# Attention and mixture-of-experts kernel: the order and the PSUM banks of the score chunks change, with the opening and the issue of some weights

## The chip, the cores and the metric

One Trainium2 chip, one core of it. The metric is device microseconds of one execution, the median over runs. TensorE is called PE here, VectorE DVE, ScalarE ACT, GpSimd POOL; SP is SyncE, which only issues DMAs. A row of weight loads has the engine name PEld: loading weights runs beside PE's matmuls.

## The reference, cut to what matters

```python
# attention: q, k, v are (4, 12, 448, 64); cap = 30
scores = (q @ k.T) / 8
scores = cap * tanh(scores / cap)
attn = exp(scores - max); attn /= attn.sum(-1) + 1e-9
x = (attn @ v)              # -> (1792, 768), the heads side by side
# mixture of experts: 8 experts, w1 (8, 768, 1024), w2 (8, 1024, 768)
logits = x @ w_gate; e = argmax(logits)
gate = softmax(logits)[e]; eom = sigmoid(x @ w_output_gate)[e]
out = gate * eom * (relu(x @ w1[e]) @ w2[e])
```

## The kernel before, in words

The work has two stages. Attention runs over NU = 24 units: a unit is two heads of one batch, six units are a batch. The experts' stage then takes blocks of 128 rows that chose one expert, and smaller "rests", through w1 and w2.

**One unit.** The 448 keys of a head are three chunks of 128 and 64 more. `qk(u, s)` for s = 0, 1, 2 makes the scores of 128 keys of both heads: 6 matmuls that use 64 rows of the array each (one head in each half of the array, three passes for the high and low parts of K and Q), into two PSUM banks. `qk(u, 3)`, the half chunk, takes the last 64 keys of both heads together: 3 matmuls over all 128 rows, one bank. ACT applies tanh to each chunk from PSUM into the SBUF tile `pt`, and then one exp over the whole tile (`expo`). `pv(u, c)` multiplies with the values, 4 pieces, into one PSUM tile `u`, which `u_evac` copies to SBUF. The kernel is a software pipeline: in the loop's turn for unit u the order is qk(u), DVE's transposes and splits of K and Q for later units (`turn_next`), part of the row sums of unit u-1 on POOL (`presum`), exp(u), pv(u-1), `sums` of units u-3 and u-2 on PE when u is odd, the copy of pv(u-1), then the rest of the row sums on POOL. Each engine works through its own instructions in the order in which they are written.

**Slots.** The router of a batch is cut into pieces (`end_of_batch`), hung into the turns of the units that follow, at the places named "f", "g", "h", "q", "e" of the loop. `gate_mm` and `gate_out` (PE, ACT), `sums_out` (ACT), `sums_tr` and `recips` (PE, DVE), `gate_tr` and `gate_mul` (PE, DVE), `logits`, `choose`, `rank_mm`, `place`, `enter`, and `rws`, which turn and store the rows of x (`row_tr` and `row_out` by PE and DVE, `row_v` by DVE alone).

**Banks.** PSUM has 8 banks. One is the tile `t` of the transposes by DVE, one is `sm` (the row sums of a batch). The other six before the change, from unit NN = 3 on: A and B of two banks each for the scores, C of one bank for the half chunk (`s3`), D of one bank for `u`. Chunks 0 and 2 go to A, chunk 1 to B; the order is 0, 1, half, 2. The router's tiles take B and C in turn (`extra`). Units 0 to 2 run on three rotating pairs of banks (tags r0 to r2) in the order 0, 1, 2, half.

```python
for s in range(NK) if u < NN else (0, 1, NK):
    qk(u, s)
...
    qk(u, NK if u < NN else 2)
```

**The copy of u.** For u >= UACT it is ACT's, after exp in its queue; for smaller u it is DVE's.

**The opening.** K and Q of units 0 to 2 are loaded in natural layout, by SP's and ACT's queue, and turned by PE (`nat_k`, `nat_q`, `first_planes`).

**Rests' weights.** Three rests have weights of their own (`OWN`), loaded by POOL's queue into buffers of their own (`rh`): after each chunk of the experts' matmuls `between` calls `pump`, which issues one such load when a buffer is free (`hraw` counts the issued, `hused` the used).

Of the kernel before, what the change touches and what calls it, by code (L numbers as in the profile page):

```python
# [9 lines left out]
F32 = mybir.dt.float32  # L10
# [12 lines left out]
def tile_kernel(ctx: ExitStack, tc, q, k, v, cap, w_gate, w_ogate, w1, w2, out):  # L23
    nc = tc.nc
    B, H, S, D = q.shape
    NT, DM = out.shape
    E, _, DFF = w1.shape
# [27 lines left out]
    WARM = (32, 7)  # L55
    RB = 7
    SP0 = 3
    UACT = 8
    TURN = {0: (0, 0), 1: (0, 0), 3: (2, 1), 5: (2, 1), 6: (2, 1), 7: (2, 1), 13: (2, 1), 19: (2, 1),
            20: (0, 0), 21: (0, 0), 22: (0, 0)}  # L60
    KD = DM // 128
# [49 lines left out]
    def load_natural(dst, src, n, m, engs, lo=0):  # L111
        for j in range(2):
            o = lo if j == 0 else 0
            engs[j].dma_start(out=dst[:, 0:n, j], in_=src[j, o:o + n * m].rearrange("(c p) d -> p c d", c=n))

    def load_nat(u, engs):
        (k0, q0), k_, q_ = nat[u], heads(k, u), heads(q, u)
        load_natural(k0, k_, NK, 128, engs, T0)
        r0, n = u * S, NP * S + SK
        engs[1].dma_start(out=k0[0:64, NK], in_=k.rearrange("b h s d -> (b h s) d")[r0:r0 + 2 * n]  # L120
                          .rearrange("(j r) d -> r j d", j=2)[0:T0])
        load_natural(q0, q_, NCH, CP, engs)

    KT, QT = (0, 1, 4), (2, 3, 5)
    kview = [raw1[i].rearrange("p (h r a) -> p h r a", h=2, a=32) for i in KT]
# [167 lines left out]
    def copy(act, dst, src):  # L293
        if act:
            nc.scalar.activation(out=dst, in_=src, func=ACTF.Copy)
        else:
            nc.vector.tensor_copy(out=dst, in_=src)
# [39 lines left out]
    def first_planes(u, mid=lambda: None):  # L337
        ts, (main, *tails) = k_parts(u, nat_k(u))
        if u:
            copy(False, main[0], main[2])  # L340
            minus(main[1], main[2], main[0])
        mid()
        q_, (q0,) = q_parts(u, nat_q(u))
        if u:
            copy(False, q0[0], q0[2])
        else:
            copy(True, main[0], main[2])
            copy(True, q0[0], q0[2])
            minus(main[1], main[2], main[0])
            scales()  # L350
        minus(q0[1], q0[2], q0[0])
        for x, z, y in tails:
            copy(False, x, y)
            minus(z, y, x)
        pl[u] = ts + q_

    def t_k(u):
        pl[u] = planes_of(k_parts(u, turned(ldk.pop(u), SK + 128)))
# [24 lines left out]

    def scores(name, z):
        ring[0] += 1
        return ps_s[0].tile([128, 2, 512], F32, tag="AB"[z] if begun else f"r{ring[0] % 3}", name=name)

    ready = {}

    def single(name, z):  # L390
        if not begun:
            return scores(name, z)[:, 0]
        return ready.pop(z, None) or ps_s[0].tile([128, 512], F32, tag="CD"[z], name=name)

    begun = []

    def fixed():
        begin.close()
        ps_s[0] = att.enter_context(tc.tile_pool(name="ps_s", reuse_waits="tile", bufs=1, space=PSUM))
        begun.append(1)  # L400
        for z in (1, 0):
            ready[z] = ps_s[0].tile([128, 512], F32, tag="CD"[z], name=("s3", "u")[z])

    spare = [0]

    def extra(name):
        spare[0] ^= 1
        return scores(name, 1)[:, 0] if spare[0] else single(name, 0)

    def nat_k(u):  # L410
        pk = tbank([128, S], "tk0")
        for c in range(NK + 1):
            n = min(128, S - c * 128)
            nc.tensor.transpose(pk[:, c * 128:c * 128 + n], nat[u][0][0:n, c].rearrange("p j d -> p (j d)"), ident[0:n, 0:n])
        return pk
# [6 lines left out]

    def qk(u, s):
        KH, KL, QH, QL = pl[u]
        if s == 0:
            pt[u] = ptp.tile([128, 2 * NK + 1, S], F32, tag="pt", name="pt")
        n = 2 if s < NK else 1
        sl = slice(s * 128, (s + 1) * 128)
        if s < NK:
            ps = scores("s", s % 2)  # L430
            for i, (x, y) in enumerate(((KH, QH), (KL, QH), (KH, QL))):
                for j in range(2):
                    h = slice(64 * j, 64 * j + 64)
                    nc.tensor.matmul(ps[:, j, 0:S], lhsT=x[h, sl], rhs=y[h], start=(i == 0), stop=(i == 2))  # L434
            ps = ps[:, :, 0:S]
        else:
            ps = ps_m.tile([128, S], F32, tag="sm", name="s3m") if u == 1 else single("s3", 0)[:, 0:S]
            for i, (x, y) in enumerate(((KH, QH), (KL, QH), (KH, QL))):
                nc.tensor.matmul(ps, lhsT=x[:, SK:], rhs=y, start=(i == 0), stop=(i == 2))
            ps = ps.unsqueeze(1)  # L440
        nc.scalar.activation(out=pt[u][:, 2 * s:2 * s + n], in_=ps, func=ACTF.Tanh, scale=icap)  # L441
# [4 lines left out]
    def pv(u, c):  # L446
        P = pt[u]
        V = vvs[u // 2 % 2][:, u % 2]
        if c == 0:
            ups[u] = (single("u", 1) if u < NU - 1 else scores("u", 1)[:, 0])[:, 0:S]  # L450
        for j in range(2):
            nc.tensor.matmul(ups[u][64 * j:64 * j + 64], lhsT=V[:, c, j, :], rhs=P[:, 2 * c + (j if c < NK else 0)],  # L452
                             start=(c == 0), stop=(c == NK))
# [49 lines left out]
    def end_of_batch(b):  # L503
        def bank(shape, name, m=False):
            if b == B - 1:
                return tbank(shape, name)
            if m:
                return ps_m.tile(shape, F32, tag="sm", name=name)
            x = extra(name)[0:shape[0], 0:math.prod(shape[1:])]
            if len(shape) == 2:  # L510
                return x
            k = "abc"[:len(shape) - 1]
            return x.rearrange(f"p ({' '.join(k)}) -> p {' '.join(k)}", **dict(zip(k, shape[1:])))
# [3 lines left out]
            nc.scalar.activation(out=ssb, in_=smt.pop(b), func=ACTF.Identity, bias=epsc)  # L517

        def sums_tr():
            ps = rt["trec"] = bank([CP, NCH, 4, 32], "trec", b == B - 2)  # L520
            for c in range(NCH):
                nc.tensor.transpose(ps[:, c].rearrange("p j n -> p (j n)"),
                                    rt["ssb"][:, c * CP:(c + 1) * CP], ident)
# [18 lines left out]
            copy(True, g, rt["tg"][0:n])  # L542

        def gate_tr(g):
            ps = rt["pg"] = bank([CP, 2, 192], "pg")
            for i in range(2):
                c = 2 * g + i
                for r in range(2):
                    n = 32 * (grp[r][1] - grp[r][0])
                    o = 32 * grp[r][0]  # L550
                    nc.tensor.transpose(ps[:, i, o:o + n], rt[f"gsb{r}"][:, c * CP:(c + 1) * CP], ident[0:n, 0:n])
# [148 lines left out]
        gts = [L(P(gate_tr, g), P(gate_mul, g)) for g in range(2)]  # L700
        g0, g1 = t[2], t[3]
        if b < B - 2:
            at = {(-2, "q"): [g0], (0, "q"): [g1], (0, "e"): [sums_out], (1, "g"): [t[1], rws[0]], (1, "e"): [recips_b],
                  (2, "e"): [rws[1]], (3, "g"): gts, (3, "e"): [rws[3]], (4, "g"): [rws[2]], (4, "h"): [logits, choose],
                  (5, "g"): [rank_mm, place, place2, rws[4]], (5, "h"): [enter], (6, "e"): [rws[5]]}
            for i, x in enumerate(((6, "g"), (8, "g"), (9, "g"), (10, "g")) if b == 0 else ((6, "g"),) * NCH):
                at.setdefault(x, []).append(P(scatter, (i,)))
        elif b == B - 2:
            g = early()
            nx = P(next, g, None)  # L710
            lds = [P(load_raw, 0, w, c) for w in range(2) for c in range((KD, KF)[w])]
            fd = [P(fetch_dma, i) for i in range(NE)]
            at = {(-2, "q"): [g0], (0, "f"): [P(sums, EARLY), g1, sums_out], (0, "h"): [t[1], *gts, logits, choose],
                  (1, "g"): [rws[0], rank_mm, place], (1, "h"): [place2, enter, scatter], (1, "q"): [rws[1], rws[2], rws[3], store_rows],
                  (2, "g"): [rws[4], rws[5]], (2, "h"): [store_rows, P(v_main, NU - 2, nc.sync), P(v_tails, NU - 2, nc.sync), *[nx] * 6, P(set_known, NE)],
                  (2, "q"): [fd[0], P(v_main, NU - 1, nc.sync), *lds[:2], fd[1]],
                  (3, "h"): [P(gather, 0), P(gather, 1), *lds[2:KD]],
                  (3, "e"): [fd[2], *lds[KD:KD + 2], fd[3]], (4, "f"): lds[KD + 2:]}
# [340 lines left out]
    for u in range(NU):  # L1059
        if u % 2 and u < NU - 3:  # L1060
            load_v(u + 1)
        if u == NN:
            fixed()
        spare[0] = 0
        for s in range(NK) if u < NN else (0, 1, NK):
            qk(u, s)
        if u > 0:
            load_ahead()
        if u == 0:
            first_planes(1, lambda: qk(0, NK))  # L1070
        else:
            qk(u, NK if u < NN else 2)
# [220 lines left out]

    def pump():

        if rsp and len(hraw) < len(hseq):
            w = hseq[len(hraw)][0]
            if sum(x[0] == w for x in hraw) - hused[w] < (KD, KF)[w]:
                load_h(len(hraw) + 1)
# [151 lines left out]
```

## Time and profile before

| | us |
|---|---|
| median of 3 runs | 499.81 (499.52 to 500.13) |
| the profiled execution | 501.27 |
| its span, first to last instruction | 499.70 |
| first exp starts (end of the opening) | 11.48 |
| exp of unit 3, 8, 14, 19 starts | 29.96, 65.16, 110.52, 149.56 |
| exp of unit 22, 23 starts | 176.01, 182.60 |
| PE busy, share of the span | 97% |
| DVE, ACT, POOL busy, share of the span | 76%, 74%, 59% |

The exps mark the units: ACT does one of 2.91 us in each, so the distance from one exp's start to the next is the length of a unit. Up to 182.60 the kernel is in attention, after that in the experts' stage.

### The profile page before, as it was taken

The numbers are of one execution on the slowest core, as the hardware profiler recorded it, in microseconds if no ns is written. First come the engines' busy times: TensorE is split into PE (matmuls) and PEld (weight loads), VectorE is DVE, ScalarE is ACT, GpSimd is POOL, SyncE is SP. The second block draws the span as 40 slices with busy tenths as digits, with TensorE's granted clock in tenths as the row PEclk, the third lists the DMA queues.
The fourth block names the chain that finished last, engine by engine and source line by source line (L and its number), as shares of the span: only waits on it lengthen the run. The fifth ranks groups of instructions, "written<-read, shape, count | busy, mean of one in ns | idle before, by whom it ended". The sixth has DMA issues, their size and how long they took to land. (4 is left out here: it accounts for less than half of the span.)

```text
span 499.7 us, 9942 instructions
## 1 busy us (share of the span) xinstructions
PE 484.3 (97%) x3040; PEld 335.9 (67%) x3040; DVE 380.4 (76%) x688; ACT 370.0 (74%) x433; POOL 296.0 (59%) x310
## 2 busy tenths in 40 slices
PE   7999999999989999999999999999999899999994
PEld 6544445445445535789998888978799667686691
DVE  6788899999978888999988969758595656565440
ACT  5999999899897797375798878857586666584551
POOL 7899999898998345573758643138356053522001
PEclk9999999999999999999999999999999999999998
DMA  7776777677573669870795263194889599791001
GB/s 175 117 140 114 125 126 136 113 133 115 106 127 55 118 184 335 275 254 1 253 391 220 95 221 134 57 361 168 281 268 407 202 355 411 272 383 46 0 34 53
DMA packets 158590, 91.95 MB, mean 184 GB/s; under 512 B 141234, under 2 KB 141370, under 8 KB 158528
## 3 DMA queue, kind: packets, MB, share of 16 engines
q1 hardware_dynamic: 148544, 58.24, 44.6%
q0 software_dynamic: 8832, 32.74, 17.7%
q8 instruction: 26, 0.43, 0.4%
q10 hardware_dynamic: 1152, 0.25, 0.2%
q14 instruction: 36, 0.29, 0.2%
HBM read 123.68 MB, written 12.04 MB: 272 GB/s over the span
## 5 line engine op out<-in xcount | busy, mean ns | idle before, releaser
L1154 DVE TENSOR_TENSOR wr<-raw,wr 128x768 fp32r<-128x768 f32 (+1 forms) x167 | 171.6, 1066 | 66.4 <-ACT wr L1153 65.6
L1153 ACT ACTIVATE wr<-raw 128x768 fp32r<-128x768 f32 (+1 forms) x167 | 150.3, 935 | 27.4 <-PE py L1175 11.0
L441 ACT ACTIVATE pt<-s,icap 128x896 f32<-128x896 f32 (+1 forms) x95 | 79.4, 917 | 9.2 <-PE s L434 8.2
L452 PE MATMUL u<-pt,vv 128*64 128x448 f32 x384 | 78.2, 546 | 0.5 <-ACT pt L444 0.3
L1175 PE MATMUL py<-wr,hh 128*128 128x384 f32 x352 | 77.3, 340 | 0.0
L1175 PE MATMUL php<-wr,xh 128*128 128x512 f32 x264 | 74.8, 405 | 0.0
L1244 POOL DMA_INDIRECT out_dram<-yo,ti x13 | 20.9, 1610 | 86.3 <-ACT yo L1242 72.3
L444 ACT ACTIVATE pt<-pt,capc 128x3136 f32<-128x3136 f32 x24 | 69.9, 2913 | 0.6
L1175 PEld LDWEIGHTS py<-wr,hh 128*128 128x128 f32 x352 | 61.2, 188 | 4.0 <-issue 3.7
L1175 PEld LDWEIGHTS php<-wr,xh 128*128 128x128 f32 x264 | 47.4, 188 | 12.8 <-issue 2.8
L452 PEld LDWEIGHTS u<-pt,vv 128*64 128x64 f32 x384 | 25.6, 136 | 40.5 <-issue 35.9
L465 POOL TENSOR_TENSOR pb<-pb,pt 64x448 f32<-64x448 f32 x40 | 45.7, 1143 | 3.1
L460 POOL TENSOR_TENSOR pb<-pt 128x896 f32<-128x896 f32 x20 | 42.3, 2113 | 7.8 <-ACT pt L444 4.1
L1175 PE MATMUL py<-wr,hl 128*128 128x384 f32 x176 | 44.8, 335 | 0.0
L461 POOL TENSOR_TENSOR pb<-pb,pt 128x896 f32<-128x896 f32 x20 | 42.1, 2105 | 1.6
L1175 PE MATMUL php<-wr,xl 128*128 128x512 f32 x132 | 41.5, 395 | 0.0
L1291 POOL DMA_DIRECT2D rh<-in_moe_w_dram x42 | 23.2, 555 | 17.3 <-DVE wr L1154 7.8
L1175 PEld LDWEIGHTS py<-wr,hl 128*128 128x128 f32 x176 | 31.8, 188 | 0.0
L1175 PEld LDWEIGHTS php<-wr,xl 128*128 128x128 f32 x132 | 24.8, 188 | 6.0
L1345 POOL DMA_INDIRECT out_dram<-yh,toh x6 | 7.8, 1300 | 34.9 <-ACT wr L1153 16.7
L953 POOL DMA_INDIRECT xg<-xs,ti x14 | 19.8, 1416 | 6.7 <-POOL ti L946 3.8
L637 POOL DMA_INDIRECT tab<-ent,posi x16 | 16.4, 1024 | 9.2 <-DVE ent L629 4.8
(334 smaller groups left out, 825.1 us busy)
## 6 DMA issues: line engine op xcount, KB each, us to landing
raw<-in_moe_w_dram SPq DMA_DIRECT2D x78, 512.0 KB
raw<-in_moe_w_dram SPq DMA_DIRECT2D x104, 384.0 KB
rh<-in_moe_w_dram POOLq DMA_DIRECT2D x18, 512.0 KB, 8.0
rh<-in_moe_w_dram POOLq DMA_DIRECT2D x24, 384.0 KB, 10.2
raw<-in_q_dram SPq DMA_DIRECT2D x45, 112.0 KB
raw<-in_k_dram SPq DMA_DIRECT2D x84, 56.0 KB
vv<-in_v_dram SPq DMA_DIRECT2D x48, 96.0 KB
xs<-xr SPq DMA_DIRECT2D x24, 112.0 KB
```

The costliest lines, as they stand in the source:

```text
L441: nc.scalar.activation(out=pt[u][:, 2 * s:2 * s + n], in_=ps, func=ACTF.Tanh, scale=icap)
L444: nc.scalar.activation(out=pt[u], in_=pt[u], func=ACTF.Exp, scale=capc)
L452: nc.tensor.matmul(ups[u][64 * j:64 * j + 64], lhsT=V[:, c, j, :], rhs=P[:, 2 * c + (j if c < NK else 0)], start=(c == 0), stop=(c == NK))
L460: eng.tensor_tensor(out=s1[u], in0=P[:, 0:2], in1=P[:, 2:4], op=ALU.add)
L461: eng.tensor_tensor(out=s1[u], in0=s1[u], in1=P[:, 4:6], op=ALU.add)
L465: eng.tensor_tensor(out=s1[u][h, j], in0=s1[u][h, j], in1=P[h, 2 * NK], op=ALU.add)
L953: nc.gpsimd.indirect_dma_start(out=g, out_offset=None, in_=xs[0:n], in_offset=bass.IndirectOffsetOnAxis(ap=ti, axis=0), bounds_check=n - 1 ...
L1153: nc.scalar.activation(out=t[:, 0, 0:F], in_=raw, func=ACTF.Copy)
L1154: nc.vector.tensor_tensor(out=t[:, 1, 0:F], in0=raw, in1=t[:, 0, 0:F].bitcast(F32), op=ALU.subtract)
L1175: nc.tensor.matmul(ps[g][:, 0:n], lhsT=st[:, c], rhs=w[:, z, g * n:(g + 1) * n], start=(c == 0 and st is hi and z == 0), stop=(c == (KD, K ...
L1244: nc.gpsimd.indirect_dma_start(out=out, out_offset=bass.IndirectOffsetOnAxis(ap=ti, axis=0), in_=y, in_offset=None, bounds_check=NT - 1, o ...
L1291: nc.gpsimd.dma_start(out=d, in_=rows_of(src, e, w, c), **kw)
```

## The change

From unit 3 on the half chunk is first and chunks 0, 1, 2 follow. The six banks are three pairs, A, B, C: the half chunk takes C, chunks 0, 1, 2 take A, B, C, and in the units of the set `BFIRST` (9 to 12, 15 to 21) B, A, C. The tile `u` of pv goes into the first bank of A (of B in the last unit). ACT copies `u` from unit 2 on instead of unit 8. The router's tiles take B; the second half of the gate transposes and all of `trec` take the bank `sm`, and in batch 2 the tiles alternate between B and `sm`. For batches 0 and 1 the gate matmuls of the first three pairs move one unit later, their copies behind the copy of u, and the gate transposes, the logits, the ranks and three of the row pieces move about one unit earlier or change places. In the opening the second half of Q is issued ahead of K's last 64 rows on ACT's queue; DVE instead of ACT makes the high part of K, and the last 64 keys are turned and split only after chunks 0 to 2 (`tail0`). `pump` issues two loads at a time once a rest has used its first w1 chunk.

```diff
     SP0 = 3
-    UACT = 8
+    UACT = 2
     TURN = {0: (0, 0), 1: (0, 0), 3: (2, 1), 5: (2, 1), 6: (2, 1), 7: (2, 1), 13: (2, 1), 19: (2, 1),
...
         r0, n = u * S, NP * S + SK
+        if u == 0:
+            load_natural(q0, q_, NCH, CP, engs)
         engs[1].dma_start(out=k0[0:64, NK], in_=k.rearrange("b h s d -> (b h s) d")[r0:r0 + 2 * n]
                           .rearrange("(j r) d -> r j d", j=2)[0:T0])
-        load_natural(q0, q_, NCH, CP, engs)
+        if u:
+            load_natural(q0, q_, NCH, CP, engs)
 
...
         else:
-            copy(True, main[0], main[2])
+            copy(False, main[0], main[2])
             copy(True, q0[0], q0[2])
             minus(main[1], main[2], main[0])
+        minus(q0[1], q0[2], q0[0])
+        if not u:
             scales()
-        minus(q0[1], q0[2], q0[0])
-        for x, z, y in tails:
+        for x, z, y in tails if u else ():
             copy(False, x, y)
...
         pl[u] = ts + q_
+
+    def tail0():
+        pk = ps_m.tile([128, S], F32, tag="sm", name="tk0t")
+        nc.tensor.transpose(pk[:, SK:S], nat[0][0][0:64, NK].rearrange("p j d -> p (j d)"), ident[0:64, 0:64])
+        hi, lo = kpl[0]
+        for j in range(2):
+            h, c = slice(64 * j, 64 * j + 64), slice(SK + 64 * j, SK + 64 * j + 64)
+            copy(False, hi[h, c], pk[h, SK:S])
+            minus(lo[h, c], pk[h, SK:S], hi[h, c])
 
...
         ring[0] += 1
-        return ps_s[0].tile([128, 2, 512], F32, tag="AB"[z] if begun else f"r{ring[0] % 3}", name=name)
-
-    ready = {}
-
-    def single(name, z):
-        if not begun:
-            return scores(name, z)[:, 0]
-        return ready.pop(z, None) or ps_s[0].tile([128, 512], F32, tag="CD"[z], name=name)
+        return ps_s[0].tile([128, 2, 512], F32, tag="ABC"[z] if begun else f"r{ring[0] % 3}", name=name)
 
...
         begun.append(1)
-        for z in (1, 0):
-            ready[z] = ps_s[0].tile([128, 512], F32, tag="CD"[z], name=("s3", "u")[z])
 
     spare = [0]
-
-    def extra(name):
-        spare[0] ^= 1
-        return scores(name, 1)[:, 0] if spare[0] else single(name, 0)
+    BFIRST = set()
+
+    def extra(name, two):
+        spare[0] ^= two
+        return ps_m.tile([128, 512], F32, tag="sm", name=name) if two and spare[0] else scores(name, 1)[:, 0]
 
...
         pk = tbank([128, S], "tk0")
-        for c in range(NK + 1):
+        for c in range(NK + (u > 0)):
             n = min(128, S - c * 128)
...
         KH, KL, QH, QL = pl[u]
-        if s == 0:
+        if u not in pt:
             pt[u] = ptp.tile([128, 2 * NK + 1, S], F32, tag="pt", name="pt")
...
         if s < NK:
-            ps = scores("s", s % 2)
+            ps = scores("s", s ^ 1 if s < 2 and u in BFIRST else s)
             for i, (x, y) in enumerate(((KH, QH), (KL, QH), (KH, QL))):
...
         else:
-            ps = ps_m.tile([128, S], F32, tag="sm", name="s3m") if u == 1 else single("s3", 0)[:, 0:S]
+            ps = ps_m.tile([128, S], F32, tag="sm", name="s3m") if u == 1 else scores("s3", 2)[:, 0, 0:S]
             for i, (x, y) in enumerate(((KH, QH), (KL, QH), (KH, QL))):
...
         if c == 0:
-            ups[u] = (single("u", 1) if u < NU - 1 else scores("u", 1)[:, 0])[:, 0:S]
+            ups[u] = scores("u", 0 if u < NU - 1 else 1)[:, 0, 0:S]
         for j in range(2):
...
                 return ps_m.tile(shape, F32, tag="sm", name=name)
-            x = extra(name)[0:shape[0], 0:math.prod(shape[1:])]
+            x = extra(name, b == B - 2 and name != "tg")[0:shape[0], 0:math.prod(shape[1:])]
             if len(shape) == 2:
...
         def sums_tr():
-            ps = rt["trec"] = bank([CP, NCH, 4, 32], "trec", b == B - 2)
+            ps = rt["trec"] = bank([CP, NCH, 4, 32], "trec", True)
             for c in range(NCH):
...
         def gate_tr(g):
-            ps = rt["pg"] = bank([CP, 2, 192], "pg")
+            ps = rt["pg"] = bank([CP, 2, 192], "pg", g == 1)
             for i in range(2):
...
         if b < B - 2:
-            at = {(-2, "q"): [g0], (0, "q"): [g1], (0, "e"): [sums_out], (1, "g"): [t[1], rws[0]], (1, "e"): [recips_b],
-                  (2, "e"): [rws[1]], (3, "g"): gts, (3, "e"): [rws[3]], (4, "g"): [rws[2]], (4, "h"): [logits, choose],
-                  (5, "g"): [rank_mm, place, place2, rws[4]], (5, "h"): [enter], (6, "e"): [rws[5]]}
+            at = {(-1, "q"): [P(gate_mm, 0)], (-1, "e"): [P(gate_out, 0)], (0, "q"): [P(gate_mm, 1)], (0, "e"): [P(gate_out, 1), sums_out],
+                  (1, "g"): [t[1], rws[0]], (1, "e"): [recips_b], (2, "g"): gts, (2, "e"): [rws[1]],
+                  (3, "g"): [rws[2]], (3, "h"): [logits, choose], (4, "g"): [rank_mm, place, place2], (4, "e"): [rws[3]],
+                  (5, "g"): [rws[4]], (5, "h"): [enter], (6, "e"): [rws[5]]}
+            BFIRST.update(NP * (b + 1) + 1 + x for x in range(2, 6))
             for i, x in enumerate(((6, "g"), (8, "g"), (9, "g"), (10, "g")) if b == 0 else ((6, "g"),) * NCH):
...
             nx = P(next, g, None)
+            BFIRST.update(NP * (b + 1) + 1 + x for x in range(3))
             lds = [P(load_raw, 0, w, c) for w in range(2) for c in range((KD, KF)[w])]
             fd = [P(fetch_dma, i) for i in range(NE)]
-            at = {(-2, "q"): [g0], (0, "f"): [P(sums, EARLY), g1, sums_out], (0, "h"): [t[1], *gts, logits, choose],
+            at = {(-1, "q"): [P(gate_mm, 0)], (-1, "e"): [P(gate_out, 0)], (0, "f"): [P(sums, EARLY), g1, sums_out], (0, "h"): [t[1], *gts, logits, choose],
                   (1, "g"): [rws[0], rank_mm, place], (1, "h"): [place2, enter, scatter], (1, "q"): [rws[1], rws[2], rws[3], store_rows],
...
             fixed()
-        spare[0] = 0
-        for s in range(NK) if u < NN else (0, 1, NK):
+        spare[0] = 1
+        for s in range(NK) if u < NN else (NK, 0, 1):
             qk(u, s)
...
         if u == 0:
+            tail0()
             first_planes(1, lambda: qk(0, NK))
...
 
-        if rsp and len(hraw) < len(hseq):
+        for _ in range(2 if hused[0] else len(rsp[:1])):
+            if len(hraw) == len(hseq):
+                return
             w = hseq[len(hraw)][0]
...
                 load_h(len(hraw) + 1)
```

## Rows read from the trace of the kernel before

**Rows 1.** Stages: from:to, length, each engine's busy us, clock, DMA.
```profile
core 0: us, PE busy (x) PEld busy (x) DVE busy (x) ACT busy (x) POOL busy (x), PEclk, DMA share, GB/s
29.96:65.16 35.20, 35.20 (x225) 16.60 (x223) 30.56 (x53) 32.56 (x29) 33.57 (x22) 1.00 0.75 128
65.16:110.52 45.36, 45.01 (x286) 21.91 (x284) 42.76 (x87) 41.24 (x41) 41.41 (x26) 1.00 0.71 126
110.52:149.56 39.04, 37.83 (x239) 17.98 (x235) 34.51 (x72) 35.15 (x35) 36.10 (x25) 1.00 0.68 115
149.56:176.01 26.45, 25.60 (x165) 13.72 (x167) 22.07 (x71) 20.55 (x22) 16.16 (x14) 1.00 0.46 84
176.01:182.60 6.59, 6.43 (x41) 3.09 (x37) 5.43 (x7) 6.56 (x7) 2.83 (x4) 1.00 0.42 113
```

**Rows 2.** Timeline of PE's weight loads, unit 3: start, us, line, tile, releaser.
```profile
25.55 0.19 PEld L434 LDWEIGHTS s<-QH,K3H 64*128 64x128 f32 x2 [0.70 <-issue]
...
26.97 0.19 PEld L439 LDWEIGHTS s<-QH,K3H 128*128 128x128 f32 x1 [0.31 <-DVE tk L310]
...
27.77 0.19 PEld L434 LDWEIGHTS s<-QH,K3H 64*128 64x128 f32 x2 [0.29 <-ACT pt L441]
...
28.57 0.20 PEld L452 LDWEIGHTS u<-pt,vv 128*64 128x64 f32 x4 [0.30 <-issue]
...
31.73 0.16 PEld L484 LDWEIGHTS sm<-pb,ohc 128*32 128x32 f32 x8 [0.70 <-issue]
32.62 0.18 PEld L434 LDWEIGHTS s<-QH,K4H 64*128 64x128 f32 x2 [0.73 <-issue]
```

**Rows 3.** Timeline of ACT, units 1, 4, 14, 22.
```profile
14.30 2.78 ACT L441 ACTIVATE pt<-s,icap 128x896 f32<-128x896 f32 x3
...
33.59 3.33 ACT L441 ACTIVATE pt<-s,icap 128x896 f32<-128x896 f32 x4 [0.73 <-PE s L434]
...
107.17 3.32 ACT L441 ACTIVATE pt<-s,icap 128x896 f32<-128x896 f32 x4
...
176.01 2.92 ACT L444 ACTIVATE pt<-pt,capc 128x3136 f32<-128x3136 f32 x1
178.83 0.52 ACT L470 ACTIVATE ut<-u 128x448 f32<-128x448 f32 x1
```

**Rows 4.** Timeline of PE's weight loads, unit 14, chunk 2.
```profile
108.23 0.18 PEld L434 LDWEIGHTS s<-QH,K4H 64*128 64x128 f32 x2 [0.53 <-ACT pt L441]
```

**Rows 5.** PE's groups by line, whole span: count, busy us, mean ns, idle before.
```profile
L646 PE MATMUL trow<-ident,ut 128*112 128x128 f32 x72 | 10.9, 279 | 0.7 <-ACT pt L441 0.4 <-DVE xr L651 0.3
...
L536 PE MATMUL tg<-ut,wg 128*32 128x448 f32 x48 | 7.5, 542 | 0.0
...
L551 PE MATMUL pg<-ident,gsb 96*112 96x96 f32 x32 | 3.8, 252 | 0.0
...
L522 PE MATMUL trec<-ident,ssb 128*112 128x128 f32 x16 | 2.5, 282 | 1.2 <-ACT ssb L517 1.2
```

**Rows 6.** Timeline of the opening, ACT's queue, DVE, PE and ACT.
```profile
2.17 0.60 ACTq L114 DMA_DIRECT2D raw<-in_q_dram  x1
...
5.11 0.17 DVE L207 MEMSET raw<- 64x128 f32 x1
...
5.68 0.56 DVE L303 TENSOR_TENSOR K0L<-tk,K0H 128x384 fp32r<-128x384 f32 x1 [0.40 <-ACT K0H L295]
...
5.72 0.58 PE L420 MATMUL tq<-ident,raw 112*128 112x112 f32 x4 [0.60 <-DMA raw<-in_q_dram]
...
6.92 0.62 DVE L303 TENSOR_TENSOR QL<-tq,QH 128x448 fp32r<-128x448 f32 x1 [0.41 <-ACT QH L295]
...
7.46 0.21 DVE L297 CAST K0H<-tk 64x64 fp32r<-64x64 f32 x1
...
8.11 3.35 ACT L441 ACTIVATE pt<-s,icap 128x896 f32<-128x896 f32 x4 [1.22 <-PE s L434]
```

**Rows 7.** Timeline of PE's weight loads, the last rest's second matmul.
```profile
453.03 0.20 PEld L1315 LDWEIGHTS pyh<-rh,hth 128*64 128x64 f32 x4 [0.51 <-DMA rh<-in_moe_w_dram]
```

## The prediction

> **What bounds the kernel now.** I read the stages first [rows 1]. In all of them PE is nearly always busy: all of 35.20 us in the stage of units 4 to 8, 45.01 of 45.36 in the next. A busy PE isn't a PE at its peak, though, and ACT (32.56 of 35.20) and POOL (33.57) stand close behind it, so a wait of a microsecond in a unit's loop moves the limit to ACT. The granted clock is 1.00 in every stage of attention, that is its upper level of 2.4 GHz, also in the one where PE waits 1.2 us for a copy [rows 1, 5]; the idle pieces that I expect below are no longer, so I keep that clock.
>
> The second view is one unit on PE [rows 2]. Chunks 0 and 1 follow each other in one shape of the array and take 26.97 - 25.55 = 1.42 us. The half chunk, with a change of shape on both sides, takes 0.80, and so does chunk 2. The values take 31.73 - 28.57 = 3.16, the row sums of every second unit 0.89. A quiet unit is 1.42 + 0.80 + 0.80 + 3.16 = 6.18 us of PE. A chunk alone costs 0.80, in a row with another 0.71 or less: of the two, one avoided change of shape is worth 2 x 0.80 - 1.42 = 0.18.
>
> The third is ACT [rows 3]. Three whole tanhs end 2.78 after the first began; one is 1.01 long, so each begins 0.89 after the last. The first tanh begins 0.97 after PE loads the first weights of its chunk (32.62 to 33.59) [rows 2, 3]. The copy of u begins 2.82 after exp began and takes 0.52. When a bank is what PE waits for, it loads within 0.05 of the release: the first tanh of unit 14 ends at 107.17 + 1.01 = 108.18, chunk 2, which wants its bank, loads at 108.23 [rows 3, 4].
>
> **The change part by part.** *Order of the chunks.* Half, 0, 1, 2 has one change of shape less: PE's quiet unit falls from 6.18 to 6.00. For units 3 to 23 that is 21 x 0.18 = 3.8 us, if PE stays the limit.
>
> *u in A.* Before, u has a bank of its own, and PE never waits for its copy. After, pv(u-1) can't start before the tanh of the chunk in A is done, and the next chunk in A can't start before ACT has copied u, which it does behind exp. The Trainium skill (Perfetto Trace Analysis, Optimizing Tensor Performance, Matmuls) says that independent groups of matmuls should rotate through different banks, so that the copying out of one overlaps the next group; this edit gives that up for u. The wait of [rows 4] shows the same effect for chunk 2.
>
> Outside BFIRST chunk 0 is in A. The loop is then exp to copy 2.82, copy 0.52, release 0.05, first tanh 0.97, three tanhs 2.78, exp again: 7.14, say 7.17 with the hand-over to exp. PE needs 6.00, or 6.89 with row sums, and fits in it: it idles 1.2 or 0.3 us, ahead of chunk 0, and ACT some 0.5 ahead of the first whole tanh. So quiet units 3 to 6 go from PE's length to 7.17. In BFIRST chunk 0 is in B and chunk 1 in A; the copy is hidden, but the values wait for the second whole tanh: half chunk 0.80, then 0.97 + 0.89 + 1.01 + 0.05 = 2.92, then 3.16, together 6.88. A row or gate transposition (0.61 and 0.95 a piece: 10.9/18 and 3.8/4) [rows 5] lies in that wait, ahead of the values, as does what is left of the three chunks, which take 1.42 + 0.80 - 0.18 = 2.04.
>
> *The copy on ACT from unit 2.* 0.52 more on ACT for units 2 to 7, inside the 7.17; what is queued behind it is the half chunk's tanh of the next unit, and PE's chunk 0 waits for it too. DVE loses a copy from a queue that was busy 30.56 of 35.20 [rows 1], so DVE's pieces come earlier; that is worth nothing while DVE isn't what ends last.
>
> *The slots.* No instruction is added, but their tiles' banks change. A gate matmul is 7.5/8 = 0.94 of PE, less what overlaps the sums, 0.9. Lengths after: unit 7 and 13 (row sums, gate matmul) 0.80 + 2.04 + 3.16 + 0.89 + 0.9 = 7.79; 8 and 14 (sums' transposition 2.5/4 = 0.63, hidden; a row transposition that wants B, so the second whole tanh) 0.80 + 2.92 + 0.61 + 3.16 = 7.49; 9 and 15 (row sums; gate transpositions behind the chunks, 2.04 + 0.95 = 2.99) 0.80 + 2.99 + 3.16 + 0.89 = 7.84; 10 and 16 6.88; 11 and 17 6.88 + 0.89 = 7.77; 12 and 18 (gate matmul) 6.88 + 0.9 = 7.78.
>
> Now by stage, against [rows 1], from exp to exp. Units 3 to 8: 4 x 7.17 + 7.79 = 36.5 for 35.20, **+1.3**. Units 8 to 14: 7.49 + 7.84 + 6.88 + 7.77 + 7.78 + 7.79 = 45.55 for 45.36; I take **+0.1**, because the 0.9s are rounded up. Units 14 to 19: 7.49 + 7.84 + 6.88 + 7.77 + 7.78 = 37.8, and exp of unit 19 about 1.0 later in its unit than a quiet one, behind two copies for the router of some 0.5 each: 38.8 for 39.04, **-0.3**. Units 19 to 22: three changes of shape less, -0.5, against a new wait of the second gate transposition, in the bank sm, for the reciprocals, up to 0.5: **-0.2**. Unit 22 to 23, quiet and without BFIRST: 7.17 for 6.59, **+0.6**. Attention from unit 3 on: +1.5. Bounds: -3.8, if all waits are covered, and +4.5, if the gate tiles in sm wait for DVE in two batches besides (below).
>
> *The opening.* The second half of Q lands 5.72 - 2.17 = 3.55 after its issue and is issued 0.7 earlier, so PE turns Q at about 5.0. DVE's last preparation ends at 5.28; then K's high part 0.56, the low part 0.56, Q's low part 0.62: 7.1 for 7.54 before, and the first tanh at 7.7 for 8.11 [rows 6]. But the last 64 keys now come behind chunks 0 to 2: these hold PE until 7.1 + 2.0 = 9.1, the transposition takes at most 0.3 (half of the 0.58 for four), four small instructions of DVE at 0.21 and some hand-over [rows 6] 1.0, the last passes of the half chunk and their way to ACT 0.8 less what overlaps: its tanh begins at 10.7 to 11.0, and exp at 11.4 to 11.65 for 11.48. I take **-0.1**; bounds -0.45 (all of the first tanh's gain stays) and +0.2. Units 1 to 3 are chained by ACT and pass this on.
>
> *Loads two by two.* They are in POOL's queue behind gathers and scatters. PE waits once visibly for such a load, 0.51 [rows 7]; the last two loads come some microseconds earlier: **-0.4**, bounds -0.7 and +0.7, where the earlier loads take the DMA engines from the blocks' weights.
>
> **Sum:** +1.5 - 0.1 - 0.4 = +1.0. The profiled execution would go from 501.27 (span 499.70, 1.57 around it) to 502.3; it lies 1.46 over the median, and on the median 499.81 + 1.0 = **500.8 us**. That is about the 0.2% (1.0 us) that a measurement of this kernel tells from no change.
>
> **The rivals.** *PE stays the limit (faster).* If ACT's copy of u is done before PE comes back to A, the loop of 7.17 never closes and every unit keeps PE's 6.00: 499.81 - 3.8 - 0.1 - 0.4 = 495.5; if it holds in half of the units, 497.7. For it: PE is busy 35.20 of 35.20 and ACT only 32.56 [rows 1], so ACT has some 0.5 us a unit to give. Against it: PE reaches chunk 0 of the next unit 0.80 + 2.04 + 3.16 = 6.0 after this one's, the release comes at 7.17. It decides from there: a release 1.2 earlier, or 1.2 of other work on PE. The Trainium skill (TensorEngine Tiling, Tiling Modes, Key Properties) states that a change of tiling mode drains the array. By that rule alone the sum is this rival's; the 0.18 of [rows 2] agrees in sign. Chance 0.24.
>
> *The bank sm holds the row sums up (slower).* In units 9 and 15 the second gate transposition takes sm, where the next batch's row sums must go 4 us later; DVE reads it behind its transposes of K and Q. DVE is busy 42.76 of 45.36 there [rows 1]. If it is 2 us behind, PE waits some 1.5 in either batch: 503.8. Against it: DVE has lost its copies and those stages gain 1.3 us of time. Chance 0.15.
>
> *The loss is taken back (no change).* POOL's sums of rows are 33.57 of 35.20 in the first stage; units slower by 0.3 let POOL and the loads of K, Q and V get ahead, and the waits for them later in attention shrink by the same 1 us: 499.8. For it: three engines within 10% of each other; against: PE has few waits of that kind to give back (45.01 of 45.36). Chance 0.11.
>
> **How the numbers follow.** My forecast has 0.50, with its own range 499.7 to 502.0; a little over half of that is more than 1.0 above, so 0.26 slower and 0.24 same. Adding the rivals: faster 0.24 and 0.01 from the edges, same 0.24 + 0.10, slower 0.26 + 0.15. The range for 8 in 10 is 498.0 to 503.0: it leaves out the full saving of the first rival and the worst of the second, and takes in the bounds of opening and loads.
>
> **What would show it.** Right: weight loads of chunk 0 in units 4 to 7 ended by ACT's copy of u, with more than 0.5 us of idle time, and some 0.5 us idle on ACT ahead of the first whole tanh; exps 7.1 to 7.3 apart there; in BFIRST units the values, or the transpositions ahead of them, waiting for a tanh; chunks 0, 1, 2 without a gap of 0.3 between them. Wrong: exps of units 3 to 8 no more than 35.3 apart; row sums of units 9 and 15 ended by DVE's gm; the first exp more than 0.4 from 11.48; PE waiting for weights in the experts' stage longer than before.

## The result, and the profile after

The median of the changed kernel is 501.69 us over 22 runs, against 499.68 us over 22 runs of the kernel before on the same chip: the medians are some 2.0 us apart. The ratio on record is 1.0051, 95% interval 1.0038 to 1.0064; it isn't formed from the two medians (their quotient is 1.0040), but it says the same: slower, by about half a per cent. The profiled execution took 500.42 us, its span is 498.7: a little shorter than the profiled execution before. The two views together say that a comparison of these two traces from end to end would mislead, so I read them stage by stage.

Unit 4, in this part, is the stretch from the exp of unit 3 to the exp of unit 4; the prediction counts the same stretch as its unit 3. Windows of the kernel after, cut at the same exps as [rows 1], with one stage ahead (from the exp of unit 2 to that of unit 3) and one behind:

```profile
core 0: us, PE busy (x) PEld busy (x) DVE busy (x) ACT busy (x) POOL busy (x), PEclk, DMA share, GB/s
23.56:30.72 7.16, 6.41 (x41) 3.30 (x39) 5.86 (x12) 6.35 (x7) 6.85 (x5) 1.00 0.73 134
30.72:66.94 36.22, 34.34 (x223) 17.05 (x221) 29.88 (x51) 34.80 (x34) 34.26 (x22) 1.00 0.75 129
66.94:112.01 45.07, 43.87 (x286) 22.46 (x284) 41.35 (x84) 42.10 (x42) 39.73 (x25) 1.00 0.72 128
112.01:150.45 38.44, 36.42 (x239) 18.23 (x235) 32.90 (x69) 35.46 (x35) 35.66 (x25) 1.00 0.75 115
150.45:176.78 26.33, 25.27 (x167) 14.26 (x169) 22.83 (x71) 20.54 (x21) 17.50 (x14) 1.00 0.53 72
176.78:183.94 7.16, 6.06 (x39) 3.15 (x37) 4.66 (x6) 6.67 (x7) 2.36 (x4) 1.00 0.38 91
183.94:498.70 314.76, 306.51 (x1909) 245.35 (x1903) 224.11 (x314) 210.33 (x280) 139.48 (x178) 1.00 0.61 223
```

The two stages of the kernel before that [rows 1] leaves out:

```profile
23.80:29.96 6.16, 6.16 (x39) 3.08 (x37) 4.93 (x10) 6.13 (x7) 5.93 (x4) 1.00 0.76 142
182.60:499.67 317.07, 307.26 (x1909) 245.34 (x1905) 223.49 (x314) 209.69 (x280) 141.76 (x178) 0.99 0.61 221
```

From the first exp (11.48 before, 11.25 after) to that of unit 23, attention went from 171.12 to 172.69 us, +1.57: +1.00 in unit 3, +1.02 in units 4 to 8, -0.29, -0.60, -0.12, and +0.57 in unit 23. PE's busy time in units 4 to 8 fell from 35.20 [rows 1] to 34.34 and its idle time rose from nothing to 1.88, while ACT is now busy 34.80 of 36.22. In the experts' stage this execution was 2.3 shorter than the one before; the experiments show that this differs from execution to execution (below).

The loop itself, on PE's weight loads of units 4 and 5 after (33.03 and 39.32 half chunk, 34.11 and 41.26 chunk 0, 36.17 values; compare [rows 2]):

```profile
33.03 0.19 PEld L444 LDWEIGHTS s<-QH,K4H 128*128 128x128 f32 x1 [0.73 <-issue]
...
34.11 0.19 PEld L439 LDWEIGHTS s<-QH,K4H 64*128 64x128 f32 x2 [0.57 <-ACT ut L475]
...
36.17 0.20 PEld L457 LDWEIGHTS u<-pt,vv 128*64 128x64 f32 x4 [0.31 <-ACT pt L446]
...
39.32 0.19 PEld L444 LDWEIGHTS s<-QH,K0H 128*128 128x128 f32 x1 [0.70 <-issue]
...
41.26 0.19 PEld L439 LDWEIGHTS s<-QH,K0H 64*128 64x128 f32 x2 [1.44 <-ACT ut L475]
```

with the matmuls of chunk 0 that these loads belong to, whose brackets are PE's own idle time:

```profile
34.11 0.47 PE L439 MATMUL s<-QH,K4H 64*128 64x448 f32 x2 [0.20 <-ACT ut L475]
...
41.27 0.47 PE L439 MATMUL s<-QH,K0H 64*128 64x448 f32 x2 [1.07 <-ACT ut L475]
```

and the same stretch on ACT (compare [rows 3]):

```profile
30.72 2.91 ACT L449 ACTIVATE pt<-pt,capc 128x3136 f32<-128x3136 f32 x1
33.53 0.52 ACT L475 ACTIVATE ut<-u 128x448 f32<-128x448 f32 x1
34.00 0.63 ACT L446 ACTIVATE pt<-s,icap 128x448 f32<-128x448 f32 x1
35.04 2.80 ACT L446 ACTIVATE pt<-s,icap 128x896 f32<-128x896 f32 x3 [0.40 <-PE s L439]
37.87 2.91 ACT L449 ACTIVATE pt<-pt,capc 128x3136 f32<-128x3136 f32 x1
...
42.18 2.80 ACT L446 ACTIVATE pt<-s,icap 128x896 f32<-128x896 f32 x3 [0.45 <-PE s L439]
```

The reader is to see the circle: exp 30.72, copy of u 33.53 (2.81 later), its end 34.05, chunk 0 at 34.11, the first whole tanh at 35.04 (0.93 later), three tanhs, exp at 37.87. That is 7.15, and it is the same in units 4 and 5, though unit 4 has row sums on PE and unit 5 has none.

### The profile page after: what moved, and what is told of

It reads as the page before. It is cut to its first block, busy times and chain, and to the rows that moved or that the text cites. A ratio compares the mean times of both kernels' runs of the same rounds, so it can differ in the third digit from the quotient of the medians.

```text
span 498.7 us, 9969 instructions
## 1 busy us (share of the span) xinstructions
PE 479.8 (96%) x3040; PEld 338.3 (68%) x3040; DVE 378.6 (76%) x683; ACT 374.0 (75%) x438; POOL 294.0 (59%) x310
## 5 line engine op out<-in xcount | busy, mean ns | idle before, releaser
L446 ACT ACTIVATE pt<-s,icap 128x896 f32<-128x896 f32 (+1 forms) x95 | 81.6, 915 | 13.0 <-PE s L444 7.4
L1253 POOL DMA_INDIRECT out_dram<-yo,ti x13 | 22.0, 1691 | 88.6 <-ACT yo L1251 83.2
L1356 POOL DMA_INDIRECT out_dram<-yh,toh x6 | 6.1, 1014 | 33.3 <-ACT wr L1162 12.7
```

The costliest lines, as they stand in the source:

```text
L1253: nc.gpsimd.indirect_dma_start(out=out, out_offset=bass.IndirectOffsetOnAxis(ap=ti, axis=0), in_=y, in_offset=None, bounds_check=NT - 1, o ...
```

## The experiments

All times are medians in us. "Exp 8" and the like are starts in the trace counted from the start of the first exp; "rest" is the span behind the exp of unit 23. In the last columns stand the ratio on record to the kernel before on the same chip (not the quotient of the medians) and its 95% interval. The runs were made on several chips, on which the kernel before has medians from 499.51 to 499.70.

| kernel | median (runs) | exp 8 | exp 14 | exp 23 | rest | ratio | interval |
|---|---|---|---|---|---|---|---|
| before, its trace | 499.51 to 499.70 | 53.68 | 99.04 | 171.12 | 317.07 | | |
| after, its trace | 501.69 (22) | 55.69 | 100.76 | 172.69 | 314.79 | 1.0051 | 1.0038 to 1.0064 |
| e1_again | 501.60 (10) | 55.68 | 100.76 | 172.72 | 315.25 | 1.0048 | 1.0033 to 1.0062 |
| e10_after_look | 501.36 (8) | 55.66 | 100.75 | 172.72 | 316.08 | 1.0036 | 1.0018 to 1.0054 |
| e12_after_look2 | 501.68 (6) | 55.65 | 100.72 | 172.70 | 315.27 | 1.0051 | 1.0032 to 1.0071 |
| e2_pump_back | 502.02 (6) | 55.69 | 100.80 | 172.76 | 316.94 | 1.0052 | 1.0034 to 1.0071 |
| e3_pump_only | 499.26 (12) | 53.74 | 99.10 | 170.58 | 314.82 | 1.0003 | 0.9991 to 1.0016 |
| e4_dve_copy | 502.35 (6) | 54.15 | 101.00 | 174.63 | 315.09 | 1.0054 | 1.0034 to 1.0073 |
| e5_no_bfirst | 507.13 (5) | 55.67 | 102.86 | 178.25 | 315.54 | 1.0153 | 1.0132 to 1.0173 |
| e6_all_bfirst | 505.25 (5) | 57.99 | 103.52 | 176.12 | 316.81 | 1.0113 | 1.0093 to 1.0133 |
| e7_before_act_copy | 499.86 (12) | 54.44 | 99.73 | 171.15 | 315.40 | 1.0007 | 0.9995 to 1.0020 |
| e8_few_dve_copies | 502.02 (12) | 54.54 | 99.64 | 170.72 | 316.55 | 1.0047 | 1.0030 to 1.0065 |
| e11_few_again | 501.14 (5) | 54.50 | 99.60 | 172.34 | 315.04 | 1.0033 | 1.0020 to 1.0045 |
| e9_other_pair | 500.37 (12) | 53.67 | 98.76 | 169.70 | 315.03 | 1.0018 | 1.0006 to 1.0030 |

**The changed kernel again: e1_again, e10_after_look, e12_after_look2.** No edit.

> The changed kernel as it is. Theory A (ACT's copy of u closes a loop of 7.16 us; the rest of the loss lies in the experts' stage and comes with the loads issued two by two): ratio 1.003 to 1.006 and single times spread over 3 us or more; exp of unit 23 within 0.1 of 183.94 in the trace, whatever the span is, so that a longer run than the first profile shows its excess behind 360 us, as waits for weights. Rival B (the excess of slow executions is spread over the whole span, or lies in attention): exp of unit 23 moves with the span.

> The changed kernel once more, for another trace and ten more times. Executions of it spread from 500.4 to 505.1, those of the kernel before from 498.2 to 501.8. Theory A (what a slow execution loses is either the weights that come late near 370 to 400 us, up to 2.2 as seen with single loads, or a fall of TensorE's clock in mid-span, 1.7 as seen once with DVE's copies): unit 23 at 172.7 after the first exp in this trace too, and any excess over 500.4 explained by these two places. Rival B: unit 23 elsewhere by 0.3 or more without a fall of the clock.

> As the look before: the changed kernel, a third trace and more times. Theory A: unit 23 at 172.7 after the first exp, the rest of attention's units within 0.1 of those of the first trace, excess over 500.4 in a fall of the clock or in late weights at 370 to 400 us. Rival B: a unit of attention longer by 0.3 or more without either.

Attention is the same within 0.03 in all four traces. The excess over the first trace lies in the opening (first exp 11.25 to 11.65) and in the rest (314.79 to 316.08). So theory A is right on attention each time, but the 0.38 by which the exp of unit 23 comes later in e1 (184.35 for 183.94) is the opening, which it didn't name. The late weights that it did name show in e10 alone, as 0.35 of idle PE at 388.72. What the longest runs, up to 505.1, lose isn't shown: none of them was traced, and none of the four traces has a fall of the clock before its last microseconds. The mean granted clock of every run says a little: it is 0.993 in the trace of e4, which has a fall in mid-span (below), and 0.995 to 0.998 in the other traces. Of the twelve runs of the changed kernel above 502.5 (of 46), three are at 0.992 or 0.993, the others at 0.994 to 0.998, so such a fall isn't what most of them lose.

**One load at a time, and two at a time: e2_pump_back, e3_pump_only.** The first puts this into the changed kernel, the second the reverse into the kernel before.

```diff
-        for _ in range(2 if hused[0] else len(rsp[:1])):
-            if len(hraw) == len(hseq):
-                return
+        if rsp and len(hraw) < len(hseq):
```

> The changed kernel with the rests' weights issued one by one, as before; nothing else is undone. Theory A: attention stays (exp of unit 23 at 183.9), the spread shrinks to that of the kernel before (under 2.7 us) and the median is 0.5 to 1.0 below the changed kernel, some 1.3 above the kernel before, ratio 1.002 to 1.003. Rival B (the loads are hidden, and the spread comes from the 1.3 us by which all of the experts' stage now stands later against the transfers): median and spread as of the changed kernel, ratio 1.004 to 1.006. Rival C (two by two helps, as the step of -0.4 in the forecast has it): 0.4 slower than the changed kernel.

> The kernel before with the rests' weights issued two by two and nothing else. Theory A: attention as before (exp of unit 23 at 182.6), the experts' stage 0.5 to 1.0 longer on the median and single times spread over 3 us or more, ratio 1.001 to 1.002. Rival B: no difference, ratio within 0.0005 of 1. Rival C (the step of -0.4): ratio 0.999.

Theory A of these two falls: two by two isn't what makes the changed kernel slower. In the medians the two pairs differ by 0.42 (with each other on one chip: 502.02 and 501.60) and 0.25, both in favour of two by two and both inside the intervals, and the ratio of e3, 1.0003, has the other sign; the forecast's -0.4 can't be told from nothing. In two of the three traces with single loads PE has a wait of over 1 us between 385 and 400 us (1.34 before, 1.57 in e2, none in e7), but so it has in traces with pairs: 1.23 in e6, 0.98 in e8, 0.35 in e10. Here PE in the experts' stage of the kernel before, in that of e2, and in that of e8:

```profile
400.01 0.44 PE L965 MATMUL pt_x<-ident,xg 128*128 128x128 f32 x2 [1.34 <-ACT xth L1020]
```

```profile
390.10 0.66 PE L973 MATMUL pt_h<-ident,h 128*128 128x128 f32 x4 [1.57 <-ACT hth L1028]
```

```profile
387.52 0.66 PE L973 MATMUL pt_h<-ident,h 128*128 128x128 f32 x4 [0.98 <-ACT hth L1028]
```

The releaser is ACT, but in e2 ACT itself was late, behind weights:

```profile
386.88 0.85 ACT L1162 ACTIVATE wr<-raw 128x768 fp32r<-128x768 f32 x1 [1.99 <-DMA raw<-in_moe_w_dram]
388.93 0.84 ACT L1162 ACTIVATE wr<-raw 128x768 fp32r<-128x768 f32 x1 [1.21 <-DMA raw<-in_moe_w_dram]
```

The rest was 317.07, 316.94 and 315.40 in the three traces with single loads and 314.79 to 316.81 in eleven with pairs. The five traces with that wait have the five longest rests, 316.08 to 317.07; the nine others lie between 314.79 and 315.54. One trace tells little here. And e3 shows an accident of the trace before: its unit 18 takes 8.52, as in e7 (8.46), where the trace before has 9.16 and PE's weight loads wait 0.43 and 0.52 for rows of V. Against e3, attention after is 2.1 longer, not 1.57.

**Who copies u: e4_dve_copy.** In the changed kernel:

```diff
-    UACT = 2
+    UACT = 8
```

> The changed kernel with DVE instead of ACT copying u for units 2 to 7, as before the change. Theory A: chunk 0 of units 4 to 8 no longer waits 1.2 us for a copy that stands behind exp; exps of units 3 to 7 come 6.2 to 6.9 apart in place of 7.16, exp of unit 8 at 63.5 to 65.5 in place of 66.94, and the median is 1.5 to 3.0 below the changed kernel. Rival D (DVE's queue is late too, since its copy stands behind transposes of K and Q): exps 7.1 or more apart, exp of unit 8 at 66.5 or later, no gain.

Both theories have a part of it. Units 4 to 8 take 6.88, 6.43, 6.88, 6.87, 7.63 for 7.15 (four times) and 7.62: the loop was ACT's copy. With unit 3's 1.00 set aside, these five units take 34.69 for 35.20 before the change; I take that for what the saved changes of shape leave once the loop is open, which wasn't tried by itself. But unit 10 takes 9.50 for 7.73, and nothing is left. PE, then DVE, in e4:

```profile
77.27 0.96 PE L489 MATMUL sm<-pb,ohc 128*32 128x448 f32 x8 [1.71 <-DVE gm L562]
```

```profile
76.11 1.01 DVE L562 TENSOR_TENSOR gm<-pg,rec 112x384 f32<-112x384 f32 x2
```

The second gate transposition lies in the bank sm until DVE has read it as gm, and the row sums want that bank. In the changed kernel gm ends at 75.15 and the row sums load at 76.64, 1.49 to spare; here DVE, with six copies more, is behind. A further 1.69 of e4's time is in unit 20 (11.30 for 9.61), where the granted clock fell. Windows of e4 ahead of the fall, in it and behind it:

```profile
146.00:153.29 7.29, 5.90 (x49) 3.42 (x49) 2.75 (x6) 6.80 (x8) 6.98 (x5) 1.00 0.59 118
153.29:156.70 3.41, 3.41 (x12) 1.20 (x10) 3.13 (x11) 0.70 (x1) 2.52 (x4) 0.50 0.04 5
156.70:160.00 3.30, 3.30 (x23) 1.97 (x21) 3.14 (x6) 1.69 (x3) 2.93 (x3) 1.00 0.02 1
```

**Chunk 0 in A everywhere, in B everywhere: e5_no_bfirst, e6_all_bfirst.**

```diff
-            ps = scores("s", s ^ 1 if s < 2 and u in BFIRST else s)
+            ps = scores("s", s ^ 1 if s < 2 and u in () else s)
```

```diff
-            ps = scores("s", s ^ 1 if s < 2 and u in BFIRST else s)
+            ps = scores("s", s ^ 1 if s < 2 else s)
```

> The changed kernel with chunk 0 in A in every unit (the set BFIRST is ignored). Theory A (the loop of 7.16 us through ACT's copy of u): units with a row piece in B get 7.6, as unit 8 has it now, the others 7.16, against 7.42, 7.73, 6.91, 7.67 for units 9 to 12; exp of unit 14 within 0.7 of where the changed kernel has it (100.76 after the first exp), median within 1.0 of the changed kernel. Rival B (BFIRST earns its place: without it the wait for the copy and that for the tanh of chunk 1 add up): some 0.4 more in each of 15 units, the median 3 us or more over the changed kernel.

> The changed kernel with chunk 0 in B and chunk 1 in A in every unit from 3 on. Theory A: the wait for the copy goes, the wait of the values for the second whole tanh comes; quiet units get 6.9 without row sums and 7.7 with them, as units 11 and 12 have it now, 7.3 on average for 7.16: exp of unit 8 at 0.3 to 0.8 later after the first exp than the 55.69 of the changed kernel, the median 0.2 to 1.0 above it. Rival B (only the copy counts): 6.9 in every quiet unit, exp of unit 8 at 54.5 after the first, the median 1.0 to 1.5 below the changed kernel.

In e5 my theory was wrong and the time of rival B right: 5.4 above the median of the changed kernel (BFIRST has 11 units, not the 15 of rival B). But of its two waits only one grew. PE's idle time ended by ACT's copy of u is 2.8 us in the whole of attention in e5 and in the changed kernel alike; what came is the wait for the tanh. Whatever goes to B on PE ahead of the values (a row piece, a gate transposition, a rank) waits for the second whole tanh, because chunk 1 is in B now, and the values come behind it: 0.78 or 0.79 of idle PE eight times from unit 9 to unit 20, where the changed kernel waits 0.20 to 0.61 for a tanh or not at all. PE in units 10 and 11 of e5:

```profile
82.41 0.65 PE L651 MATMUL trow<-ident,ut 128*112 128x128 f32 x4 [0.78 <-ACT pt L446]
...
89.84 0.18 PE L602 MATMUL trk<-ohb,tri 112*112 112x32 bf16 x1 [0.78 <-ACT pt L446]
```

In e6 the sign was right and the size wrong. Units 4 and 5 take 7.75 and 6.85, 7.30 on average as expected; units 6 and 7 take 7.73 each (7.15 before the edit) and units 8 and 14 8.47 and 8.48 (7.62). I read it so that with the values late, whatever else a unit has on PE comes on top instead of into the wait; that wasn't tried by itself.

**Half of the edit in the kernel before: e7_before_act_copy.**

```diff
-    UACT = 8
+    UACT = 2
```

> The kernel before with ACT copying u from unit 2 on, and nothing else of the change: u has its own bank, so no loop closes. Theory A: half of the 2.0 us that units 3 to 8 lost is ACT's own time: units without row sums go from 6.2 to 6.7 (0.52 more on ACT, whose tanhs and exp take 6.16), units with them stay; exp of unit 8 at 54.3 to 55.0 after the first exp for 53.68, and the median 0.3 to 1.0 above the kernel before, unless what was gained by DVE is worth as much later. Rival B (the copy alone costs nothing; the bank alone closes the loop): exp of unit 8 within 0.2 of 53.7 after the first. Rival C (copy alone costs all): 55.5 or later.

Theory A: exp 8 comes 0.76 later with ACT's copy alone, u in a bank of its own; units 5 and 7 go from 6.17 and 6.30 to 6.59, and PE waits for no copy of u in units 4 to 8. Against e3, 0.57 of it is left at unit 23; the median moves by 0.2, inside the interval. So the copy by ACT alone costs 0.76 of the 2.0 that units 3 to 8 lost, and with 6.59 to 7.04 in units 4, 5 and 7 there is no loop of 7.15: that takes copy and shared bank together. (The order of the chunks is the old one here; the changed kernel with u in a bank of its own wasn't tried.)

**Few copies on DVE: e8_few_dve_copies, e11_few_again.**

```diff
-    UACT = 2
+    UACT = 5
...
-        if u >= UACT:
+        if u >= UACT and u != 21:
```

> The changed kernel with DVE copying u of units 2 to 4 and of unit 21, ACT the others. What stands behind it: with DVE copying units 2 to 7 units 4 to 8 were 1.5 shorter, but DVE was 2 us late with gm, the row sums of unit 9 waited 1.71 for the bank sm, and all was lost again. Theory A (DVE's queue is what takes the gain back): with three copies fewer on DVE the wait of the row sums is under 0.4, units 4 to 6 keep 0.9 to 1.3, unit 23 is 0.4 to 0.8 shorter, and the median is 1.0 to 2.0 below the changed kernel, about that of the kernel before. Rival B (some other limit, POOL's sums at 6.83 a unit or the loads of K and Q, takes it back): exp of unit 14 again at 100.7 or later after the first exp, no row sums waiting for gm, and at most 0.6 below the changed kernel.

> The kernel with few DVE copies once more. Its trace has attention 2.0 shorter than the changed kernel, its median is no lower: 502.0 for 501.7, with single times from 499.3 to 504.3. Theory A (the execution that was profiled was one of the quick ones; the others have a fall of the clock or late weights more often): median 501 to 502.5 again, and in the trace unit 23 at 170.7 after the first exp, or later by a fall of the clock. Rival B (the attention of unprofiled executions is longer by something that this trace shows): unit 23 later than 171 without a fall. Rival C (the first median was off): median 499.5 to 500.5.

The trace of e8 has what theory A wanted: no row sums waiting for gm, 1.15 won by unit 8 and kept to unit 14 (1.12), another 1.00 in unit 23. Attention is as short as in e3. The median isn't: 502.02. The second trace shows one reason, and rival B of e11 is right as far as one trace goes: exp 23 came at 172.34 without a fall of the clock. DVE's row piece in e8, then in e11:

```profile
142.69 0.69 DVE L656 TENSOR_TENSOR xr<-trow,rec 112x512 f32<-112x512 f32 x1 [2.22 <-DMA xs<-xr]
```

```profile
142.90 0.69 DVE L656 TENSOR_TENSOR xr<-trow,rec 112x512 f32<-112x512 f32 x1 [2.90 <-DMA xs<-xr]
...
170.24 0.69 DVE L656 TENSOR_TENSOR xr<-trow,rec 112x512 f32<-112x512 f32 x1 [1.36 <-DMA xs<-xr]
```

and PE in e11, late for it twice (0.72 in unit 19, 0.97 in unit 23, with no gap of 0.3 on DVE between 170.24 and that copy of u):

```profile
143.64 0.95 PE L541 MATMUL tg<-ut,wg 128*32 128x448 f32 x6 [0.72 <-DVE xr L656]
...
179.82 0.47 PE L439 MATMUL s<-QH,K3H 64*128 64x448 f32 x2 [0.97 <-DVE ut L477]
```

DVE waits for the store of earlier rows to leave its buffer, by an amount that differs from execution to execution (in the four traces of the changed kernel these row pieces don't wait for a store). It reaches PE in two ways: in unit 19, where ACT copies u, because the gate matmul wants the bank B that DVE's row piece still reads; in unit 23 through DVE's copy of u.

**Another pair at unit 3: e9_other_pair.** On top of e8:

```diff
         begun.append(1)
+        for z in (1, 2, 0):
+            ready[z] = ps_s[0].tile([128, 2, 512], F32, tag="ABC"[z], name=("s1", "s2", "s3")[z])
...
         ring[0] += 1
+        if z in ready:
+            return ready.pop(z)
```

> The kernel with few DVE copies (units 2 to 4 and 21), and besides the pairs of banks changed round at unit 3, so that its half chunk no longer falls on the bank that u of unit 1 has just been written to. What stands behind it: unit 3 took 7.15 for 6.16 before, and the half chunk's first weights wait for DVE's copy of that u. Theory A: unit 3 takes 6.2 to 6.5, 0.7 to 0.9 less, and the median falls by as much against the kernel with few DVE copies. Rival B (POOL or DVE take it back by unit 14): exp of unit 14 within 0.2 of 99.64 after the first exp all the same.

Theory A: unit 3 takes 6.31, and the 0.83 are kept to unit 14 and beyond. The half chunk of unit 3, after and in e9:

```profile
26.14 0.19 PEld L444 LDWEIGHTS s<-QH,K3H 128*128 128x128 f32 x1 [1.53 <-DVE ut L477]
```

```profile
25.32 0.19 PEld L449 LDWEIGHTS s<-QH,K3H 128*128 128x128 f32 x1 [0.70 <-issue]
```

The median fell by 0.8 against e11 and 1.0 to 1.3 against the changed kernel on the same chip. Its trace is the shortest of all (span 496.0, execution 497.63 us), yet over twelve runs it is still 0.18% slower than the kernel before. No version beats the kernel before by more than its interval.

## Why the prediction was right, and where its terms were off

The forecast case happened: +2.0 measured, +1.0 forecast, 501.69 for 500.8 and inside the range. The mechanism was right as well, but the sum has only half of the loss: attention lost 0.6 more than was worked out, and the 0.5 credited to opening and loads isn't shown by any run.

*The loop through A.* Right in place and size. 7.17 was worked out, 7.14 to 7.16 came in units 4 to 7 and in unit 23; chunk 0 waits for ACT's copy of u there, by 1.07 us of idle PE in unit 5 (1.2 said) and 0.20 in unit 4 (0.3 said), and ACT idles 0.40 and 0.45 (some 0.5 said). e4 and e7 show the cause: with DVE's copy in the changed kernel, or with ACT's copy and a bank of its own in the kernel before, there is no loop of 7.15. In e8 DVE's copy of one u takes unit 23 from 7.16 to 6.16.

*Unit 3* was left out: the stages of [rows 1] that I summed over begin at its exp, and I let units 1 to 3 pass on the opening. It costs 1.00, because the half chunk, now first, falls on the bank pair into which u of unit 1 has just been written; e9 takes 0.83 of it away by another pair. This is the largest error of the sum.

*The other stages*, forecast and trace of after against e3, which does without the accident in unit 18: units 4 to 8 +1.3 and +1.0, 9 to 14 +0.1 and -0.3, 15 to 19 -0.3 and 0.0, 20 to 22 -0.2 and -0.1, 23 +0.6 and +0.6. Unit by unit the lengths came within 0.17: for units 8 to 14 here (7 to 13 in the prediction's count) 7.79, 7.49, 7.84, 6.88, 7.77, 7.78 and 7.79 were worked out, and 7.63, 7.42, 7.73, 6.91, 7.67, 7.72 and 7.62 came, six of the seven a little shorter than worked out. With unit 3 attention lost 2.1, for the +1.5 forecast: the 1.0 left out in unit 3 is partly covered by 0.7 too much in units 4 to 14.

*The opening*: -0.1 was forecast. The first exp starts at 11.23 to 11.25 in three of the eleven traces with the new opening, at 11.43 in one and at 11.63 to 11.65 in seven; with the old one at 11.39, 11.48 and 11.57 in three. So it came mostly 0.1 to 0.2 later, not earlier.

*The loads*: worth between nothing and the 0.4 said. [rows 7] was read for too much: its 0.51 is idle time of the weight load, and PE's matmuls of that rest have no gap of 0.2 there. It is gone from the trace after, but from that of e7 too, which issues the loads one by one.

*PE stays the limit* fell: PE has its 0.86 of busy time less in units 4 to 8, and waits. The rule of the Trainium skill (TensorEngine Tiling, Tiling Modes, Key Properties), that a change of tiling mode drains the array, agrees in sign with that busy time; it says nothing of who waits for whom, which decides here. (The case of this rival with half of the units adds up to 497.4, not 497.7.) *The bank sm* didn't happen after, with 1.49 us to spare, but did in e4, by 1.71 for the 1.5 priced. *The loss is taken back* fell: no wait later in attention shrank by as much.

Open: in the traces of e8 and e9 attention is 0.4 and 1.4 shorter than in that of before, and yet their medians are longer. So no run shows the median of the changed kernel fall by as much as the opened loop saves in the trace; e9 comes nearest, with 1.0 to 1.3 of the 3.0 that its attention is shorter. The late row stores of e11, the wait for weights near 390 us and the fall of the clock in e4 are three ways in which other executions lose it. How often the first two happen in a run without a trace isn't shown; a mean clock of 0.993 or less, as in e4, stands in one of the 12 runs of e8 and in one of the 12 of e9.

## What to carry to other kernels

Ask of a shared bank not only whether the reader is quick, but behind what its instruction stands in its queue: a copy of 0.52 us cost 1.0 a unit here, because it came behind an exp of 2.9, and the matmul that waited for it feeds the next exp. A saving on the busiest engine (0.18 a unit) is worth nothing once a loop over two engines is longer than that engine's work. And one trace against one trace gave -1.0 where 22 runs against 22 gave +2.0: compare stages, and take each kernel's trace more than once.

## What the runs showed of the hardware that was not expected

TensorE's granted clock fell from its upper level, 2.4 GHz, to 1.2 GHz for 3.41 us in the middle of attention in e4 (0.50 in the windows above), after 7.29 us in which PE was busy 5.90 and had idled 1.17 and 0.22 at a stretch. The changed kernel has the same gaps at the same place in its four traces, without a fall, so the clock of 1.00 that the prediction kept for attention came true there. PE's values of that unit took 4.92 for 3.23, and the unit 1.69 more.

In the opening the same transposes of Q (four matmuls) take 0.55 us in the trace after and 0.95 in e1, and the first whole tanh starts at 7.55 and 7.96, with the same program ahead of them; the granted clock reads 1.00 in both. It is 0.95 in all seven traces whose first exp starts at 11.63 or later. What makes them slower stays open.
